# Reordering the matmul steps of a fused attention and FFN kernel's forward stage, and moving one weight load

## The chip, the cores and the metric

One NeuronCore of a Trainium2 chip runs the whole program. The metric is the device time of one execution in microseconds (us). The kernel before was run three times: 1677.09, 1677.39 and 1687.07 us, median 1677.39 us.

## The reference

The program computes a transformer block with attention and a gated FFN in parallel, and all its gradients. Sequence length S = 2048, width D = 448, 16 heads of 28, FFN width F = 1792, all in bf16.

```python
def _fwd_reference(A_x, A_wqkv, A_wo, B_x, B_w_gate, B_w_up, B_w_down):
    x = A_x
    xn = layernorm(x)
    # attention: softmax(q k^T * 28**-0.5) v, then @ wo ; FFN: (silu(xn@w_gate) * (xn@w_up)) @ w_down
    return x + attention(xn, A_wqkv, A_wo) + ffn(xn, B_w_gate, B_w_up, B_w_down)

_out, _vjp = jax.vjp(_f, A_x, A_wqkv, A_wo, B_w_gate, B_w_up, B_w_down)
_grads = _vjp(grad_out)
return (_out, *_grads)        # output 0, and the six gradients as outputs 1 to 6
```

## The kernel before

**Stages.** A short prologue normalises x and projects q, k, v of the first head group. Then comes the forward stage, which is what the change touches. A second stage computes the attention gradients and, between them, the output rows and the input gradients. A short last stage finishes the gradient of x.

**The forward stage** is a list of 256 steps, `(g, qc, kt)`: 4 groups of 4 heads, 4 blocks of 512 queries (`qc`), 16 tiles of 128 keys (`kt`). In each step TensorE makes the scores of one key tile for the four heads as two *score pairs* (L531; each pair is two matmuls that use 32 rows of the array and run at the same time). ScalarE takes the exponential of each pair (L535). A pair's scores lie in one of two PSUM buffers `s_ps`, so a pair must wait for the exponential of the pair two before it. The *weighted sum* `pv(i)` (L504 to L515) is four matmuls of 32 output rows that run at the same time and accumulate exp(scores) times v in `o_ps`, of which there is one buffer. At the last key tile `pv` calls `o_items` (L420), which has VectorE copy `o_ps` to `o_raw` (L423) and puts two jobs at the front of the filler queue: four transposes of `o_raw` (`tr`, L432) and the matmuls of `do` (L454).

**Fillers.** All other matmuls of this stage wait in a queue of jobs, each a list of (cost, function) pairs; the costs are constants of the source (0.216 for a matmul of 512 columns, 0.19 for 448). `fill(budget)` takes items in order until the budget is used up. At each step `pace` is the cost still in the queue divided by the number of steps left. The queue holds the FFN: 14 blocks `fc` of 128 FFN columns, each in 4 parts `sc` of 512 rows. A part runs the jobs `a` (4 matmuls, then tanh on ScalarE at L349 and three VectorE operations), `u` (4 matmuls, then two VectorE operations, L363 and L365), in parts 1 to 3 one weight gradient `dW` of the block before (16 matmuls), and `dh` (4 matmuls, then two VectorE operations at L373, a transpose DMA on SP and three writes to `hd_d` on the POOL queue, L378). Behind the FFN block come `weight_layout` calls (L250), which transpose weights through one staging tile; four of the twelve read `wq_sb`, the layout of w_qkv in the tile `W`. Projections for the next head group go to the front of the queue at `qc == 2`. All these jobs use three PSUM buffers `f_ps` in turn.

**The order of one step before**: score pair 0, fillers for 0.45 of the pace, score pair 1, `pv` of the step before, fillers for 0.55 of the pace. At `kt == 1` the `pv` is put off, so that `kt == 2` runs two of them; this leaves `o_raw` time to be copied.

**The load of w_down.** `load_w("wd", 1)` allocates the tile `W` again (the pool has one buffer) and issues one DMA of 1568 KB on the POOL queue (L493). Before, this is called at step 224, the first of `qc == 2` of the last group (L522). The tile is first read in the second stage by the first output row (L658).

Each engine runs its own instructions in program order, and so do the DMA queues of SP and POOL.

Of the kernel before, what the change touches and what calls it, by code (L numbers as in the profile page):

```python
# [22 lines left out]
G = 4  # L23
# [14 lines left out]
def kernel(  # L38
# [145 lines left out]
    def sp_layouts(g):  # L184
        for tq, dst in ((0, spq_d), (1, spk_d)):
            s_ = stg.tile([P, NT, P], BF16, name="sp_stage")
            sp.dma_start_transpose(out=s_[:], in_=qk_tiles[(g, tq)][:])
            pool.dma_start(out=dst[g], in_=s_[:].rearrange("p t c -> p (t c)"))
# [61 lines left out]
    def weight_layout(c, i):  # L250

        d0, dn = DCH[c]
        s_ = stg.tile([P, NT, P], BF16, name="sp_stage")
        n = NFC if i < 2 else 3 * G
        src = ((B_w_gate, B_w_up)[i][d0:d0 + dn, :] if i < 2
               else wq_sb[:dn, c].rearrange("p t g r -> p (t g r)"))
        sp.dma_start_transpose(out=s_[:, :n, :dn], in_=src)
        dst = wT_d[i] if i < 2 else wqT_d
        pool.dma_start(out=dst[:, :, d0:d0 + dn], in_=s_[:, :n, :dn])
# [6 lines left out]
    def fill(budget):  # L266

        while budget > 0.05:
            if not cur:
                if not queue:  # L270
                    return
                cur.extend(queue.popleft())
            cost, fn = cur.popleft()
            fn()
            budget -= cost
            left[0] -= cost

    def push(jobs, front=False):
        left[0] += sum(c for job in jobs for c, _ in job)
        if front:  # L280
            queue.extendleft(reversed(jobs))
        else:
            queue.extend(jobs)

    def proj_items(g):
        out = []
        for tq in range(3):
            for sc in range(4):
                box = {}

                def go(c, tq=tq, sc=sc, box=box):
                    if c == 0:
                        box["m"] = proj_unit(g, tq, sc, "dve")
                    box["m"](c)
                out.append([(MM, lambda c=c, go=go: go(c)) for c in range(4)])
        out.append([(0.0, lambda: proj_done(g))])
        return out
# [3 lines left out]
    def dW_items(fc):  # L301

        out = []
        for wi in range(3):
            box = {}

            def go(t, wi=wi, box=box):
                src = ffn[fc]
                if t == 0:
                    box["ps"] = ps_f.tile([P, 512], FP32, name="f_ps")  # L310
                acc = box["ps"]
                rhs = dy_sp if wi == 0 else xn_sp
                pe.matmul(acc[:, :D], lhsT=src[:, 12 * (t // 4) + 4 * wi + t % 4, :], rhs=rhs[:, t, :D],  # L313
                          start=(t == 0), stop=(t == NT - 1))
                if t < NT - 1:
                    return
                if wi == 0:
                    o = ftmp.tile([P, D], BF16, name="dwd_sb")
                    dve.tensor_copy(out=o[:], in_=acc[:, :D])
                    pool.dma_start(out=out_6[fc * P:(fc + 1) * P, :], in_=o[:])  # L320
                else:
                    w = dwT[wi - 1]
                    dve.tensor_copy(out=w[:, :D], in_=acc[:, :D])
                    o = ftmp.tile([P, 4, P], BF16, name="dw_o")
                    sp.dma_start_transpose(out=o[:], in_=w[:])
                    dst = (out_4 if wi == 1 else out_5)[:, fc * P:(fc + 1) * P]
                    pool.dma_start(out=dst[0:384].rearrange("(c p) f -> p c f", p=P), in_=o[:, 0:3, :])
                    pool.dma_start(out=dst[384:448], in_=o[:64, 3, :])
            out.append([(MMD, lambda t=t, go=go: go(t)) for t in range(NT)])
        return out  # L330
# [54 lines left out]
    ffn_list = []  # L385
    pend = []
    for fc in range(NFC):
        nxt = dW_items(fc)
        for sc in range(4):
            ffn_list += ffn_items(fc, sc, pend[sc - 1:sc] if sc else [])  # L390
        if 0 < fc < 13:
            ffn_list.append([(0.0, lambda k=fc - 1: weight_layout(k // 3, k % 3))])
        pend = nxt
    ffn_list += pend
    push(ffn_list)
# [87 lines left out]
    wtile = {}  # L483

    def load_w(nm, parts):

        t = wp.tile([P, NFC, D], BF16, name="W")
        src = {"wd": B_w_down.rearrange("(fc p) d -> p fc d", p=P), "wg": wT_d[0], "wu": wT_d[1], "wq": wqT_d}[nm]
        n = 3 * G if nm == "wq" else NFC
        wtile[nm] = t  # L490
        step = n // parts
        q = pool if nm == "wd" else sp
        out = [lambda i=i: q.dma_start(out=t[:, i:i + step, :], in_=src[:, i:i + step, :])  # L493
               for i in range(0, n, step)]
        return out
# [6 lines left out]
    pv_next = [0]  # L502

    def pv(i):  # L504
        g, qc, kt = steps[i]
        if kt == 0:
            o_cur["o"] = ps_o.tile([P, 512], FP32, name="o_ps")
        o_ps, v = o_cur["o"], v_tiles[g]
        e = eTs.pop(i)
        for hh in range(4):  # L510
            pe.matmul(o_ps[HP * hh:HP * (hh + 1), :], lhsT=v[:, kt, HP * hh:HP * (hh + 1)],  # L511
                      rhs=e[hh // 2][:, hh % 2, :], start=(kt == 0), stop=(kt == NT - 1),
                      tile_position=(0, HP * hh), skip_group_check=True)
        if kt == NT - 1:
            o_items(g, qc, o_ps)  # L515

    for i, (g, qc, kt) in enumerate(steps):
        if kt == 0 and qc == 1:
            push([[(0.0, lambda g=g: sp_layouts(g))]], front=True)
        if kt == 0 and qc == 2 and g + 1 < G:  # L520
            push(proj_items(g + 1), front=True)
        if kt == 0 and qc == 2 and g + 1 == G:  # L522
            load_w("wd", 1)[0]()
        qT, kT = qk_tiles[(g, 0)], qk_tiles[(g, 1)]
        pace = left[0] / (nst - i)
        eTs[i] = []
        for half in range(2):
            s_ps = ps_s.tile([P, 2, 512], FP32, name="s_ps")
            for j in range(2):
                r = HP * (2 * half + j)  # L530
                pe.matmul(s_ps[:, j, :], lhsT=kT[r:r + HP, kt * P:(kt + 1) * P],  # L531
                          rhs=qT[r:r + HP, qc * 512:(qc + 1) * 512],
                          start=True, stop=True, tile_position=(r, 0))
            e = ep.tile([P, 2, 512], BF16, name="eT")
            act.activation(out=e[:], in_=s_ps[:], func=ACT.Exp, scale=SCALE)  # L535
            eTs[i].append(e)
            if half == 0:
                fill(0.45 * pace)
            else:
                if i >= 1 and kt != 1:  # L540
                    while pv_next[0] <= i - 1:
                        pv(pv_next[0])
                        pv_next[0] += 1
                fill(0.55 * pace)
    while pv_next[0] < nst:
        pv(pv_next[0])
        pv_next[0] += 1
    fill(1e9)
    fst.close()
    bst.close()  # L550

# [401 lines left out]
```

## Time and profile before

| what | value |
|---|---|
| median of three runs | 1677.39 us |
| the profiled execution: time / span | 1683.64 us / 1681.9 us |
| mean granted TensorE clock | 0.952 |
| forward stage, first to last score pair | 49.5 to 751.1 us |
| exponentials of the forward stage (L535) | 512 of 1025 ns |
| TensorE busy, all | 1519.8 us (90%) |
| ScalarE busy, all | 1186.3 us (71%) |
| VectorE busy, all | 1131.8 us (67%) |

The span is what the profiler covers; 1.7 us of the execution's time lie around it. The clock is the share of full speed that TensorE was granted. TensorE's busy time is modelled and overlaps, so that starts of instructions say more than their durations: below, the distance from the start of one group of matmuls to the start of the next is what a group costs.

### The profile page before, as it was taken

To read this page: it belongs to the slowest core of one execution; us is meant where nothing else is said; L and a number is where in the kernel's file an instruction comes from. 1 tells how busy PE (TensorE), PEld (TensorE's weight loads), DVE (VectorE), ACT (ScalarE), POOL (GpSimd) and SP (SyncE) were. 2 spreads that over 40 slices of the span, in tenths; PEclk is the share of its full clock that TensorE was granted. 3 is DMA by queue.
4 is the path that set the end of the run, shared out by engine and by line. 5 is a ranking of instruction groups with operands and counts; after the bars stand their busy time and mean duration, and the time that the engine had idled before them with its cause. 6 is when DMAs were issued, how large, how long until landed. Compare 5 with 4: busy or idle time off the path is not lost. (4 is left out here: it accounts for less than half of the span.)

```text
span 1681.9 us, 32121 instructions
## 1 busy us (share of the span) xinstructions
PE 1519.8 (90%) x12176; PEld 600.7 (36%) x12176; DVE 1131.8 (67%) x1530; ACT 1186.3 (71%) x1346; POOL 400.9 (24%) x664
## 2 busy tenths in 40 slices
PE   3699999999999999696998999999989999999875
PEld 1132333333233333232443335443335433544352
DVE  6365555555555456345887788888878888888736
ACT  2497888888777678574776777777777777777611
POOL 4133334344234333421001101010102101111132
PEclk9699999999998899797999989999999999999998
DMA  4785658687866577548999999999999999999963
GB/s 126 145 181 115 133 121 169 140 169 118 157 131 130 124 136 148 138 93 231 214 208 212 196 175 196 207 196 208 206 202 194 202 202 179 175 195 195 175 239 100
DMA packets 682155, 285.13 MB, mean 170 GB/s; under 512 B 637792, under 2 KB 651088, under 8 KB 682000
## 3 DMA queue, kind: packets, MB, share of 16 engines
q1 hardware_dynamic: 653616, 215.74, 68.7%
q0 software_dynamic: 25808, 64.30, 15.4%
q10 hardware_dynamic: 2576, 3.04, 0.6%
q8 instruction: 95, 1.56, 0.4%
q14 instruction: 60, 0.49, 0.1%
HBM read 67.34 MB, written 63.44 MB: 78 GB/s over the span
## 5 line engine op out<-in xcount | busy, mean ns | idle before, releaser
L831 DVE TENSOR_TENSOR ds<-sd,E 128x1024 bf16<-128x1024 f32 x512 | 607.6, 1217 | 81.5 <-PE sd L814 34.2
L819 ACT ACTIVATE E<-sd 128x1024 bf16<-128x1024 f32 x512 | 520.1, 1031 | 193.4 <-PE sd L814 99.0
L535 ACT ACTIVATE eT<-s_ps 128x1024 bf16<-128x1024 f32 x512 | 518.2, 1025 | 159.8 <-PE s_ps L531 154.5
L801 PE MATMUL sd<-KV,QD 32*128 32x512 bf16 x1024 | 202.1, 391 | 19.2 <-DVE ds L831 8.1
L814 PE MATMUL sd<-KV,QD 32*128 32x512 bf16 x1024 | 202.9, 388 | 10.9 <-DVE ds L831 6.8
L694 PE MATMUL acc<-ds,Qsp 128*32 128x512 bf16 x1024 | 204.5, 395 | 1.2 <-DVE ds L831 1.2
L531 PE MATMUL s_ps<-qT,kT 32*128 32x512 bf16 x1024 | 204.7, 397 | 0.0
L694 PE MATMUL acc<-E,dOsp 128*32 128x512 bf16 x1024 | 204.3, 395 | 0.0
L339 PE MATMUL f_ps<-xnT,wgu 128*128 128x512 bf16 x448 | 135.9, 400 | 24.7 <-DVE w_sb L365 13.0
L378 POOL DMA_DIRECT2D hd_d<-fT x168 | 126.9, 769 | 40.9 <-DVE fT L363 24.9
L531 PEld LDWEIGHTS <-kT 32*128 32x128 bf16 x1024 | 48.2, 91 | 203.7 <-issue 201.7
L664 PE MATMUL aux<-W,ck 128*128 128x448 bf16 x448 | 106.6, 354 | 6.9 <-DVE dsT L730 6.9
L313 PE MATMUL f_ps<-xn_sp,f_sp 128*128 128x448 bf16 x448 | 110.6, 355 | 0.0
L709 POOL DMA_DIRECT2D dqkv_d<-dkv_o x64 | 39.2, 617 | 284.9 <-ACT dkv_o L700 284.8
L801 PEld LDWEIGHTS <-QD 32*128 32x128 bf16 x1024 | 50.2, 91 | 149.0 <-issue 140.5
L511 PE MATMUL o_ps<-eT,v_sp 128*32 128x512 bf16 x1024 | 101.7, 399 | 0.0
L730 DVE COPY dsT<-aux 128x512 bf16<-128x512 bf16 x128 | 54.3, 424 | 61.7 <-ACT dsT L728 61.7
L694 PEld LDWEIGHTS <-dOsp 128*32 128x32 bf16 x1024 | 50.3, 94 | 120.3 <-issue 117.3
L814 PEld LDWEIGHTS <-QD 32*128 32x128 bf16 x1024 | 69.4, 91 | 53.4 <-issue 34.2
L721 PE MATMUL aux<-ident_bf,ds 128*128 128x128 bf16 x1024 | 78.5, 219 | 11.0 <-DVE dq_acc L758 3.5
L743 PE MATMUL aux<-dsT,Ksp 128*32 128x512 bf16 x1024 | 78.3, 405 | 4.1 <-DMA dsT<-ds 2.5
L351 DVE SCALAR_TENSOR_TENSOR g<-t_sb,f_ps 128x512 f32<-128x512 f32 x56 | 38.4, 686 | 64.6 <-ACT t_sb L349 64.5
(130 smaller groups left out, 1803.1 us busy)
## 6 DMA issues: line engine op xcount, KB each, us to landing
hd_d<-fT POOLq DMA_DIRECT2D x168, 128.0 KB, 4.0
ck<-hd_d SPq DMA_DIRECT2D x32, 448.0 KB, 4.2
ck<-hd_d SPq DMA_DIRECT2D x16, 576.0 KB, 5.0
dsT<-ds SPq DMA_TRANSPOSE x384, 4.1
dq_c<-dqkv_d SPq DMA_DIRECT2D x8, 768.0 KB, 4.7
dqkv_d<-dkv_o POOLq DMA_DIRECT2D x64, 64.0 KB, 3.5
W<-wT_d SPq DMA_DIRECT2D x14, 224.0 KB, 3.9
out_dram<-dw_o POOLq DMA_DIRECT2D x28, 96.0 KB, 4.1
```

Of the source, the lines that this page charges most:

```text
L313: pe.matmul(acc[:, :D], lhsT=src[:, 12 * (t // 4) + 4 * wi + t % 4, :], rhs=rhs[:, t, :D], start=(t == 0), stop=(t == NT - 1))
L339: pe.matmul(st[name][:], lhsT=w(c), rhs=src[:, tsl, c, :], start=(c == 0), stop=(c == 3))
L378: pool.dma_start(out=hd_d[tsl, :, G + NFC * wi + fc, :].rearrange("k p s -> p k s"), in_=o[:, wi, :].rearrange("p (k s) -> p k s", k=4))
L511: pe.matmul(o_ps[HP * hh:HP * (hh + 1), :], lhsT=v[:, kt, HP * hh:HP * (hh + 1)], rhs=e[hh // 2][:, hh % 2, :], start=(kt == 0), stop=(kt ...
L531: pe.matmul(s_ps[:, j, :], lhsT=kT[r:r + HP, kt * P:(kt + 1) * P], rhs=qT[r:r + HP, qc * 512:(qc + 1) * 512], start=True, stop=True, tile_ ...
L535: act.activation(out=e[:], in_=s_ps[:], func=ACT.Exp, scale=SCALE)
L664: return [lambda n=n: pe.matmul(ps[:, :D], lhsT=t[:, n, :], rhs=w[:, n, :], start=(n == 0), stop=(n == NFC - 1)) for n in range(NFC)]
L694: pe.matmul(acc[r:r + HP, :], lhsT=src[:, qt, 64 * hp + HP * j:64 * hp + HP * j + HP], rhs=m[:, j, :], start=(qt == 0), stop=(qt == NT - 1 ...
L801: pe.matmul(s_ps[:, j, :], lhsT=q[HP * j:HP * j + HP, qt * P:(qt + 1) * P], rhs=kv[HP * j:HP * j + HP, kc * 512:(kc + 1) * 512], start=Tru ...
L814: pe.matmul(d_ps[:, j, :], lhsT=q[r:r + HP, qt * P:(qt + 1) * P], rhs=kv[r:r + HP, kc * 512:(kc + 1) * 512], start=True, stop=True, tile_p ...
L819: act.activation(out=E[k][:], in_=s_ps[:], func=ACT.Exp, scale=SCALE)
L831: dve.tensor_tensor(out=DS[k - 1][:], in0=d_ps[:], in1=E[k - 1][:], op=ALU.mult)
```

## The change

A forward step becomes: score pair 0, `pv` of two steps before, score pair 1, then all fillers of the step in one call `fill(pace)`. The special case at `kt == 1` is gone; the last two `pv` run after the loop. The load of w_down is no longer called at step 224 but is an item of cost 0 in the filler queue, behind the last FFN block's last `dh` and ahead of that block's three `dW` jobs.

```diff
@@ -390,6 +390,8 @@
             ffn_list += ffn_items(fc, sc, pend[sc - 1:sc] if sc else [])
         if 0 < fc < 13:
             ffn_list.append([(0.0, lambda k=fc - 1: weight_layout(k // 3, k % 3))])
+        if fc == 13:
+            ffn_list.append([(0.0, lambda: load_w("wd", 1)[0]())])
         pend = nxt
     ffn_list += pend
     push(ffn_list)
@@ -519,8 +521,6 @@
             push([[(0.0, lambda g=g: sp_layouts(g))]], front=True)
         if kt == 0 and qc == 2 and g + 1 < G:
             push(proj_items(g + 1), front=True)
-        if kt == 0 and qc == 2 and g + 1 == G:
-            load_w("wd", 1)[0]()
         qT, kT = qk_tiles[(g, 0)], qk_tiles[(g, 1)]
         pace = left[0] / (nst - i)
         eTs[i] = []
@@ -534,18 +534,15 @@
             e = ep.tile([P, 2, 512], BF16, name="eT")
             act.activation(out=e[:], in_=s_ps[:], func=ACT.Exp, scale=SCALE)
             eTs[i].append(e)
-            if half == 0:
-                fill(0.45 * pace)
-            else:
-                if i >= 1 and kt != 1:
-                    while pv_next[0] <= i - 1:
-                        pv(pv_next[0])
-                        pv_next[0] += 1
-                fill(0.55 * pace)
+            if half == 0 and i >= 2:
+                pv(i - 2)
+        pv_next[0] = max(0, i - 1)
+        fill(pace)
     while pv_next[0] < nst:
         pv(pv_next[0])
         pv_next[0] += 1
     fill(1e9)
+    assert 'wd' in wtile
     fst.close()
     bst.close()
```

## The prediction

> **What bounds the kernel now.** I began with the page's table of 40 slices: TensorE is at 9 tenths in nearly all of the forward stage, with a drop in the 17th slice, and its granted clock dips there too. Then I read who waited for whom on TensorE from 60 to 720 us, which names every hole of that stage.
>
> ```profile
> PE   3699999999999999696998999999989999999875
> PEclk9699999999998899797999989999999999999998
> PE f_ps L339 <- DVE w_sb L365: 13.0, 2, 12.8
> PE f_ps L432 <- DVE o_raw L423: 11.1, 6, 3.2
> PE f_ps L313 <- DMA f_sp<-fT: 2.9, 1, 2.9
> ```
>
> So apart from its start this stage is one unbroken row of matmuls with 27 us of holes, 12.8 of them in one. No score pair ever waited for ScalarE. A step is then as long as its matmuls and whatever lies between them. TensorE's timeline shows one step, from a score pair 0 to the next; the first column is the start:
>
> ```profile
> 670.53 0.39 PE L531 MATMUL s_ps<-qT,kT 32*128 32x512 bf16 x2
> 670.85 0.82 PE L339 MATMUL f_ps<-dyT,wdT 128*128 128x512 bf16 x3
> 671.61 0.39 PE L531 MATMUL s_ps<-qT,kT 32*128 32x512 bf16 x2
> 671.92 0.40 PE L511 MATMUL o_ps<-eT,v_sp 128*32 128x512 bf16 x4
> 672.25 1.04 PE L339 MATMUL f_ps<-xnT,wgu 128*128 128x512 bf16 x4
> 673.23 0.39 PE L531 MATMUL s_ps<-qT,kT 32*128 32x512 bf16 x2
> ...
> 784.65 0.39 PE L694 MATMUL acc<-E,dOsp 128*32 128x512 bf16 x2
> 784.98 0.39 PE L801 MATMUL sd<-KV,QD 32*128 32x512 bf16 x2
> ```
>
> From start to start the runs take 0.32, 0.76, 0.31, 0.33 and 0.98 us. Three filler matmuls take 0.76 and four 0.98, so one matmul is about 0.215 us and each run pays some 0.115 us besides, whatever its length: 0.76 - 3 x 0.215. A pair or a `pv` runs as one such matmul at a time and pays the same (0.32 - 0.215). The last two lines, from the second stage, are the only neighbours like the new `pv` followed by a score pair: 0.33 us, the same again.
>
> The big hole is read on three engines' timelines; the bracket is the idle time before the instruction and what ended it:
>
> ```profile
> 689.37 1.11 POOL L493 DMA_DIRECT2D W<-in_B_w_down_dram  x1 [31.00 <-DMA sp_stage<-W]
> 699.96 0.69 DVE L363 SCALAR_TENSOR_TENSOR fT<-g,f_ps 128x512 bf16<-128x512 f32 x1 [13.40 <-DMA hd_d<-fT]
> 701.30 1.87 PE L339 MATMUL f_ps<-xnT,wgu 128*128 128x512 bf16 x4 [12.81 <-DVE w_sb L365]
> ```
>
> The load of w_down stands on the POOL queue from step 224 on, but may not overwrite `W` until the last `weight_layout` has read it, which SP does only at 684.87. For 31 us the `hd_d` writes queued behind it don't go, the three `fT` buffers fill, VectorE stops at L363, the `f_ps` buffer isn't freed and TensorE stops.
>
> **The change part by part.** The sum is made against the profiled 1683.6 us, 0.4% above the median 1677.4; a saving of this size is the same on either.
>
> *Runs of matmuls.* By the code, a step before has five runs (four at the 16 steps with `kt == 1`, and at the first): 256 x 5 - 17 = 1263. After, it has four, less the two first `pv`: 1022. The matmuls themselves are the same. 241 x 0.115 = 27.7 us less. From the spread of the starts (0.10 to 0.12) it is 24 to 29 us. [...]
>
> *The hole.* With the load behind the last `dh`, step 250 by a walk through the filler queue with the source's costs, the last reader of `W` is some 14 steps in the past, and nothing blocks POOL. 12.8 us go, and with them the slow clock after it: the clock rows read 0.50 from 691 us and 1.00 again from 708, so about 6 us of matmuls ran at half speed, 2.9 us. Next late there would be nothing that TensorE shows: its next wait is 0.6 us at 740. I take 15.7 us; a shorter wait on a busy queue would leave 10, a smoother stage after it give 18.
>
> *The load itself.* It is queued on POOL behind the last three `hd_d` writes (2.2 us) and the `dw_o` writes before them, issues in 1.1 us, and lands 8.4 us later (its row in the DMA list). Behind it waits the `dwd_sb` write, for whose buffer nobody is in a hurry. Six steps of 2.6 us and the 24 us from the last score pair (751.1) to the first matmul with `W` (774.9) are 40 us against 12: nothing, by 27 us. If that cover were gone, each us late would be a us of TensorE in the second stage's start.
>
> *ScalarE.* Two exponentials now come close together. Back to back, two take 1.93 and three 2.86 us, so 0.93 each; with one tanh (0.5) in 4.4 steps ScalarE needs 2.0 us a step. The shortest new step, with the early pace of 1.07 by the code (five filler matmuls), is 0.32 + 0.33 + 0.32 + 0.115 + 5 x 0.215 = 2.16 us. ScalarE stays just behind TensorE: +1 us (0 to 4). Were each exponential to cost its 1.025 us alone, ScalarE would need 2.17 and the first 100 steps would gain nothing: +11.
>
> *tanh.* This is what the change adds. tanh follows both exponentials of its step on ScalarE's queue; before, an `a` that ended in the first portion had its tanh between them. Counted from the start of score pair 0: the pair is done at 0.4, the exponentials end near 1.5 (0.1 on, 1.02 long) and 2.45 (0.93 more), tanh near 3.0, and VectorE's five operations, 0.6 to 0.7 us apart, near 6.4. Behind these stand two waits of TensorE.
>
> First, at the end of each query block `o_raw` (0.68 us) is queued on VectorE behind what `a`, `u` and `dh` left there, and `tr` waits for it. Before, the six waits in the stage come to 11.1 us. By the same walk I looked at which job lies ahead of `tr` at each of the 15 boundaries. After the change an `a` ends one to two steps ahead at steps 32, 48, 80, 112, 160 and 224, where `tr` waits 2.5, 2.5, 2.1, 2.0, 1.1 and 2.0 us; at 96 a `dh` and a projection make it 1.0; the others have a `dW` ahead and wait 0 to 0.3, 1.1 in all. That is 14.2 us, 3 more; step 192 and 208, which cost 3.2 and 2.7 before, become free.
>
> Such a wait also costs clock. These rows are stretches of 1 us: length, TensorE busy, clock:
>
> ```profile
> 510.00:511.00 1.00, 1.00 (x7) 1.00 1.08 187
> 511.00:512.00 1.00, 0.04 (x1) 1.00 0.86 149
> 512.00:513.00 1.00, 0.10 (x1) 0.87 1.04 179
> 513.00:514.00 1.00, 1.00 (x4) 0.50 1.58 311
> 522.00:523.00 1.00, 1.00 (x4) 0.51 0.93 212
> ```
>
> A wait of 1.86 us and then 10 us at half speed: 5 us lost. Read the same way, the waits at 146, 467, 561 and 610 us lost 3.5, 1.5, 4.5 and 1.6, so 3.2 on average with this one. Five such before, six after: +3.2. [...] Together +6 us; if these waits fall as well as they can, -13; if three more boundaries wait, +20.
>
> Second, part 0 of an FFN block has no `dW` between its `u` and the next part's `u`, which needs the same `f_ps` buffer. Twelve matmuls lie between; with VectorE done at 6.4 us the walk gives three waits of 0.3 to 0.4 us: +1.5 (0 to 8).
>
> Sum: -27.7 - 15.7 + 1 + 6 + 1.5 = -34.9 us. 1677.4 - 34.9 = 1642.5; I say 1643.
>
> **Rivals.** (1) *ScalarE or a returning block takes a part*: exponentials don't overlap (+11), or POOL blocks elsewhere and the hole stays (+15.7; a 5.2 us wait of VectorE for `hd_d` at 455 us, with no w_down load near, shows that it can). 1654 to 1658. (2) *A `pv` between two score pairs pays the price of two runs*: removing one run then saves nothing, and only the hole goes, less the new waits: -15.7 + 8.5, 1670. Against it stands the equal 0.115 at all five places of the step and at the pair of the second stage. (3) *Slower: TensorE waits for VectorE behind the later tanh in every FFN block.* A wait costs 2 us and 3.2 of clock, 5.2. Thirteen block starts would cost 68, less the 1.5 counted: 1643 + 66 = 1709. It decides from seven such waits on (34.9 / 5.2). For it: the wait of 0.18 us that the trace shows at 650 for L339 on L365, so the margin before was near nothing; against it: three of thirteen by the walk, and short. (4) *It doesn't do what it says*: the load still waits, now at the end of the stage, on something that I don't see. It would then delay the second stage's start only beyond 27 us.
>
> **How the numbers follow.** The forecast, with its bounds (1630 to 1653), 0.57; rival 1, 0.15; rival 2, 0.17; rival 3, 0.09; rival 4, 0.02. About 1% (16.8 us) is what a measurement of this kernel can tell from no change. Faster by over 1% is the forecast and rival 1: 0.72. Within 1%: rival 2, half of rival 4: 0.18. Slower: rival 3 and the rest: 0.10. For 8 in 10 the range goes from 1630 to 1670, with rivals 1 and most of 2 in it; some 0.05 lie below, 0.14 above.
>
> **What would show it.** Right: four runs a step with about 0.115 us each, `pv` to score pair in 0.33; no wait of POOL at L493 and no hole near 690; last score pair near 716 us; the second stage as long as before; L432 waits of some 14 us at the boundaries named. Wrong: score pairs or `pv` that wait for the exponential, L339 waiting for L365 in most blocks, the first matmul with `W` waiting for its load, or a clock below 0.95 in the forward stage.

## The result, and the profile after

The changed kernel takes 1652.5 us (median of six runs, 1644.9 to 1664.6) where the kernel before takes 1679.8 (six runs). The ratio is 0.983, 95% interval 0.980 to 0.986, so 28 us less (23 to 33), 1.7%. Forecast were 34.9 us less and a time of 1643, with bounds from 1630 to 1653: the time lies at the upper bound, and a fifth of the forecast saving is missing.

The page of the changed kernel, its row of TensorE and of the granted clock, in 40 slices of its 1653.5 us span:

```profile
PE   3699999999999999969998989999989899999884
PEclk9799999999999999979999989999999999999888
```

The drop in the 17th slice is gone; the one in the 18th is the change of stage. Where the forward stage begins and ends is in the answer on the score pairs: the line gives the count, the shortest, median and longest duration in ns, and the first and last start.

```profile
L531 PE MATMUL s_ps<-qT,kT x1024: 384/385/605, 49.6 to 716.6; 32*128 32x512 bf16 x171
```

The last pair starts at 716.6 instead of 751.1 us, 34.5 less; the forecast was near 716. One step, on TensorE's timeline:

```profile
655.82 0.39 PE L531 MATMUL s_ps<-qT,kT 32*128 32x512 bf16 x2
656.14 0.40 PE L513 MATMUL o_ps<-eT,v_sp 128*32 128x512 bf16 x4
656.47 0.39 PE L531 MATMUL s_ps<-qT,kT 32*128 32x512 bf16 x2
656.79 1.04 PE L339 MATMUL f_ps<-xnT,wgu 128*128 128x512 bf16 x4
657.67 0.92 PE L313 MATMUL f_ps<-xn_sp,f_sp 128*128 128x448 bf16 x4
658.52 0.39 PE L531 MATMUL s_ps<-qT,kT 32*128 32x512 bf16 x2
```

Four runs, from start to start 0.32, 0.33, 0.32 and 1.73 us. The `pv` between two score pairs costs 0.33, as its neighbour in the second stage did. In this step only a change between kinds of matmul has the price: from the four matmuls of L339 to those of L313, which use the array in the same shape (128*128), it is 0.88 us, hardly more than 4 x 0.215, so both together are one run. Who waited on TensorE, from 60 to 716 us (total, times, longest):

```profile
PE f_ps L434 <- DVE o_raw L425: 11.0, 8, 2.2
PE f_ps L339 <- DVE w_sb L365: 8.6, 4, 4.1
PE f_ps L313 <- DMA f_sp<-fT: 5.2, 2, 2.8
```

(The transposes `tr` are L434 now, `o_raw` L425.) The waits for `o_raw` are as large as before, and elsewhere; L339 and L313 wait longer than forecast. The load of w_down does as forecast: on the POOL queue it starts without a wait, and its first use comes 35 us later.

```profile
705.16 1.10 POOL L495 DMA_DIRECT2D W<-in_B_w_down_dram  x1
740.42 0.58 PE L655 MATMUL aux<-W,ck 128*128 128x448 bf16 x1
```

For all kernels below, the forward stage is taken apart in the same way: when the last score pair starts; TensorE's idle time from 72 us to then; and the time lost to the clock, which is TensorE's busy time in each us times one less the granted clock. The runs are counted by the code. The kernels ran on three chips, on which the median of the kernel before was 1679.2 to 1681.8 us.

| kernel (label) | last pair | idle | lost to the clock | runs | median | ratio to before (interval) |
|---|---|---|---|---|---|---|
| before | 751.1 | 27.7 | 26.1 | 1263 | 1679.8 | |
| changed | 716.6 | 24.8 | 18.4 | 1022 | 1652.5 | 0.983 (0.980 to 0.986) |
| changed, again (c1) | 733.2 | 25.3 | 37.1 | 1022 | 1651.9 | 0.981 (0.976 to 0.985) |
| load moved only (e1) | 734.0 | 13.2 | 22.9 | 1263 | 1666.7 | 0.991 (0.988 to 0.993) |
| new steps, load at step 228 (e2) | 734.5 | 36.5 | 24.9 | 1022 | 1668.7 | 0.992 (0.989 to 0.994) |
| tr and do later (e3) | 697.6 | 16.8 | 7.2 | 1022 | 1629.9 | 0.971 (0.965 to 0.976) |
| five runs (e4) | 734.1 | 17.0 | 17.0 | 1278 | 1666.8 | 0.990 (0.986 to 0.993) |
| lag of one (e5) | 738.2 | 33.3 | 30.9 | 1023 | 1671.8 | 0.994 (0.991 to 0.996) |
| four fT (e6) | 713.2 | 17.3 | 23.6 | 1022 | 1642.8 | 0.977 (0.972 to 0.981) |
| e3 and e6 together (e7) | 690.9 | 11.7 | 5.5 | 1022 | 1620.8 | 0.964 (0.960 to 0.967) |
| e7 again (c2) | 689.1 | 11.3 | 4.9 | 1022 | 1625.9 | 0.969 (0.966 to 0.973) |
| e7, five runs (e8) | 706.1 | 1.8 | 3.6 | 1278 | 1638.4 | 0.976 (0.973 to 0.979) |
| old steps, moved, tr later (e9) | 710.3 | 4.3 | 7.9 | 1263 | 1642.3 | 0.977 (0.972 to 0.982) |

First pair to last, the stage fell from 701.6 to 667.0 us in the two profiles, by 34.6: 2.9 less idle, 7.7 less lost to the clock, and the other 24.0 for 241 fewer runs, 0.100 each. How exact such a remainder is, two executions of the changed kernel tell (changed and c1): the second's stage is 17.0 us longer, idle time and clock account for 19.2, and 2.2 us are left over, which is 0.009 us a run.

### The profile page after: what moved, and what is told of

Read it like the earlier page. It is cut to its first block, busy times and chain, and to the rows that moved or that the text cites. A ratio compares the mean times of both kernels' runs of the same rounds, so it can differ in the third digit from the quotient of the medians.

```text
span 1653.5 us, 32129 instructions
## 1 busy us (share of the span) xinstructions
PE 1489.1 (90%) x12176; PEld 620.8 (38%) x12176; DVE 1130.9 (68%) x1530; ACT 1167.4 (71%) x1346; POOL 400.7 (24%) x664
## 4 chain that ended last, share of the span: by engine, by line
PE 60%; DMA 12%; DVE 11%; ACT 8%; issue 6%; SPq 2%; POOL 1%; DVEq 0%; POOLq 0%; ACTq 0%
PE s_ps L531 9%; PE f_ps L313 8%; PE f_ps L339 8%; DMA dsT<-ds 7%; PE sd L798 5%; ACT E L816 5%; DVE ds L828 5%; PE o_ps L513 5%; PE aux L661 5%; PE acc L691 4%; PE aux L740 4%; PE aux L655 3%; PE f_ps L157 3%; PE sd L811 2%; ACT dsT L725 2%
## 5 line engine op out<-in xcount | busy, mean ns | idle before, releaser
L535 ACT ACTIVATE eT<-s_ps 128x1024 bf16<-128x1024 f32 x512 | 497.1, 1022 | 132.0 <-PE s_ps L531 130.4
L339 PE MATMUL f_ps<-xnT,wgu 128*128 128x512 bf16 x448 | 122.8, 391 | 20.4 <-DMA wd<-in_B_w_down_dram 11.8
L313 PE MATMUL f_ps<-xn_sp,f_sp 128*128 128x448 bf16 x448 | 101.6, 359 | 0.0
L718 PE MATMUL aux<-ident_bf,ds 128*128 128x128 bf16 x1024 | 78.6, 220 | 11.7 <-DVE dq_acc L752 4.3
L313 PEld LDWEIGHTS <-f_sp 128*128 128x128 bf16 x672 | 58.5, 98 | 73.5 <-issue 23.4
```

The source lines that it names most:

```text
L339: pe.matmul(st[name][:], lhsT=w(c), rhs=src[:, tsl, c, :], start=(c == 0), stop=(c == 3))
```

## Experiments on the two halves of the change

**The load alone (e1).** The steps of the kernel before, with this:

```diff
+        if fc == 13:
+            ffn_list.append([(0.0, lambda: load_w("wd", 1)[0]())])
...
-        if kt == 0 and qc == 2 and g + 1 == G:
-            load_w("wd", 1)[0]()
```

> The steps of the kernel before, with only the load of w_down moved behind the last FFN block's dh. My theory: POOL no longer waits 31 us at the load, the hole of 12.8 us before L339 and some 3 us of half clock after it go, the last score pair of the forward stage starts near 735.5 us instead of 751.1, and the time falls by 15.7 us (10 to 18). Rival: the hole was slack for what comes next, so other waits of TensorE take its place and the time falls by less than 6 us.

The last score pair came at 734.0, 17.1 us earlier; the time fell by 16 us (ratio 0.991, interval 0.988 to 0.993). Idle time fell by 14.5. The hole was a loss of its own and nothing else took its place. The rival falls.

**The steps, with the load where it blocks (e2).** The changed kernel, with the load taken out of the queue and called at a step:

```diff
-        if fc == 13:
-            ffn_list.append([(0.0, lambda: load_w("wd", 1)[0]())])
...
+        if i == 228:
+            load_w("wd", 1)[0]()
```

> The new steps, with the load of w_down called at the start of step 228, where the filler queue stands about where it stood at step 224 before (part 1 of FFN block 12 just begun). My theory: POOL blocks again until the last weight_layout has read W, TensorE gets a hole of some 12 us near 660 to 680 us, and the time is 12 to 18 us above that of the changed kernel, some 12 to 19 below before. Rival: if the runs of matmuls save nothing and all the gain is the hole's, this is as slow as before.

16 us above the changed kernel by the medians, and 14 below before. The block and the hole are back, on POOL's and TensorE's timelines:

```profile
672.02 1.11 POOL L493 DMA_DIRECT2D W<-in_B_w_down_dram  x1 [25.21 <-DMA sp_stage<-W]
```
```profile
683.32 1.87 PE L339 MATMUL f_ps<-xnT,wgu 128*128 128x512 bf16 x4 [11.71 <-DVE w_sb L365]
```

The rival falls. So each half is worth about as much as the other, and they add: -16 and -14 against -28. The load at step 224 itself wasn't tried with the new steps. By the walk through the queue, four parts of FFN block 12 would then still lie between TensorE and the last `weight_layout`, and there are three `fT` buffers: the load and the fillers would wait for each other. That is worked out from the code and not shown by a run; by it the new steps need the load some steps later than before, as here, or moved.

**Five runs again (e4).** The fillers split in two, everything else as changed:

```diff
-            if half == 0 and i >= 2:
-                pv(i - 2)
+            if half == 0:
+                fill(0.45 * pace)
+                if i >= 2:
+                    pv(i - 2)
...
-        fill(pace)
+        fill(0.55 * pace)
```

> The changed kernel, with the fillers split again into 0.45 and 0.55 of the pace: score pair 0, fillers, pv of two steps before, score pair 1, fillers: five runs a step instead of four, with the lag, the place of the load and the matmuls of the changed kernel. My theory: 256 more runs at 0.115 us, 29 us, less up to 8 us because tanh stands between the two exponentials again: 20 to 30 us above the changed kernel, near that of the move alone less nothing. Rival: the price is not per run but the gain comes from the lag of two steps or from the one portion's bookkeeping: within 6 us of the changed kernel.

14 us above the changed kernel by the medians: neither in my range nor in the rival's. The table tells why. First pair to last took 684.8 us against 667.0, 17.8 more, though idle time was 7.8 and the loss to the clock 1.4 lower. Without those the 256 runs cost 27.0 us, 0.105 each, a little under the 0.115 that I held. What I had too small is what the split gives back: fewer waits.

**The same with few waits (e8, e9).** e8 is e7 (below) with the edit of e4. e9 is e1 with `tr` and `do` put off as in e3.

> The kernel with late tr and do and four fT buffers, its fillers split again: five runs a step instead of four. With few waits left, little clock is lost by chance, so the difference shows the price of a run. By the two kernels with many waits it is 0.10 us: 255 runs, 24 to 29 us above the kernel with four runs, 1645 to 1650. Rival: that price was an accident of the waits and the clock, and the difference is under 10 us.

> The old steps (five runs, lag of one, double pv at kt 2) with the load moved and with tr and do two steps later. Against the new steps with late tr and do (1629.9 us) it has 241 runs more: 24 to 29 us above it, 1654 to 1659. Rival: the old order leaves more time to VectorE and has so few waits left that the new order gains less than 15 us over it.

> The kernel with late tr and do and four fT buffers once more, for these comparisons on one chip: 1617 to 1625 us, with a spread of its runs under 8 us because few waits are left.

By the medians e8 is 12 us above c2 on the same chip, and e9 16; against e3, on another chip, e9 is 12 above. e8 lies between my expectation and its rival's; e9 against e3 is what its rival said: the old order has fewer waits left. c2 lies just above its expected range, at 1625.9 us, and scatters by 10 us, not under 8. Again the idle time differs the other way: e8's forward stage has almost no idle time, 1.8 us against 11.3. First pair to last, e8 took 656.7 us and c2 640.4; with idle time and clock set equal the 256 runs cost 16.3 + 9.5 + 1.3 = 27.1 us, 0.106 each. For e9 against e3 it is 661.7 - 647.5 + 12.5 - 0.7 = 26.0 for 241, 0.108. Changed against e1 gives 17.4 + 11.6 - 4.5 = 24.5, 0.102. Four comparisons, 0.102 to 0.108 us a run, with 0.100 for the change itself: that price is settled to about 0.01. In each of the four pairs four runs a step also leave 8 to 13 us more idle time than five, so three tenths to a half of what the runs save is given back in waits.

## Experiments on the waits

**tr and do two steps later (e3).** `o_items` no longer pushes its jobs, but notes them for the step after next:

```diff
-        push([...] + (dwo_items(g) if qc == 3 else []), front=True)
+        late.append((step_now[0] + 2, jobs_o))
...
+        step_now[0] = i
+        while late and late[0][0] <= i:
+            push(late.pop(0)[1], front=True)
```

> The changed kernel, with the jobs tr, do and dwo put into the filler queue two steps later than o_items is called, so that o_raw has been copied when tr is reached. My theory: the waits of L434 on o_raw (11.8 us in nine) all but go, and with them the half clock after those above 1.2 us, so the time falls by 18 to 24 us against the changed kernel. Rival A: the half clock has other causes, and only the idle 11 us go. Rival B: VectorE's backlog is the limit, and the wait appears elsewhere (score pairs, pv, L339): less than 4 us.

1629.9 us, 21 (by the ratios) to 23 us (by the medians) below the changed kernel. TensorE's waits from 70 to 697 us in this kernel:

```profile
PE f_ps L339 <- DVE w_sb L365: 5.1, 3, 4.1
PE f_ps L313 <- DMA f_sp<-fT: 4.0, 2, 2.6
PE f_ps L157 <- DVE w_sb L365: 2.5, 1, 2.5
PE o_ps L515 <- DVE o_raw L425: 2.1, 3, 0.8
```

The line for `tr` is no longer there; 2.1 us of it moved to `pv`, which needs the `o_ps` buffer that `o_raw` is copied from. Against the first profile of the changed kernel idle time fell by 8.0 us and the loss to the clock by 11.2 (29.9 against its repeat, c1). Rival A, that only the idle time goes, falls: here the waits cost more in clock than in idle time. Rival B falls too.

**Four fT buffers (e6), and both (e7).** `fT` from three buffers to four, `eT` from seven to five for the space.

> The changed kernel with four fT buffers instead of three (and five eT buffers instead of seven, for the space; a lag of two steps needs five). My theory: the two holes of about 4 us before L339 come from VectorE waiting at L363 for an fT buffer whose DMAs are late, and go; 8 us of idle time and 3 to 5 of half clock, 8 to 13 us below the changed kernel. Rival: the late DMAs only block something else a little later: less than 4 us.

1642.8 us, 9 below the changed kernel beside it (c1). That is in the expected range, but the runs alone don't show it: four runs of each scatter by 12 and 24 us, and the two intervals in the table overlap. What the fourth buffer takes away is seen in the changed kernel on VectorE and then TensorE:

```profile
453.80 0.69 DVE L363 SCALAR_TENSOR_TENSOR fT<-g,f_ps 128x512 bf16<-128x512 f32 x1 [4.46 <-DMA hd_d<-fT]
```
```profile
455.14 1.01 PE L339 MATMUL f_ps<-xnT,wgu 128*128 128x512 bf16 x2 [4.14 <-DVE w_sb L365]
```

VectorE stands at L363 for a free `fT` buffer whose write to `hd_d` hasn't landed (in the other hole, up to 91.97 us, it waits 5.47 us for the transpose into `f_sp`), keeps its `f_ps` buffer, and TensorE stops: the chain of the w_down hole, but from DMAs that are merely late. With four buffers L339 waits less:

```profile
PE f_ps L434 <- DVE o_raw L425: 11.6, 8, 2.2
PE f_ps L313 <- DMA f_sp<-fT: 5.0, 3, 2.6
PE f_ps L339 <- DVE w_sb L365: 0.7, 2, 0.4
```

> Both: tr and do two steps later, and four fT buffers. If the two kinds of waits are independent, the gains add: 18 to 22 us from the first (measured) and 8 to 13 from the second, 1617 to 1625 us. If they share a cause in VectorE's backlog, no better than 1628.

1620.8 us, and 1625.9 on another chip: the fastest here, 3.1 to 3.6% below before (ratios 0.969 and 0.964 with the intervals of the table) where the change alone is 1.7 to 1.9% below. That is what independent gains would give, but no proof of it: on top of e3 the fourth buffer brought 4 to 9 us by the medians, within the scatter.

**A lag of one step (e5).** `pv(i - 1)` in the place of `pv(i - 2)`.

> The changed kernel with pv of one step before instead of two. pv then stands 0.32 us into a step and needs the second exponential of the step before, which ends near 2.45 us after that step's start, while early steps are 2.2 us long. My theory: pv waits 0.1 to 0.4 us in most of the first 100 steps and after each tanh, hardly in the last 100: 8 to 25 us above the changed kernel. Rival: ScalarE is never late, the lag of two steps buys nothing: within 4 us.

20 us slower than the changed kernel beside it, inside my range, but not by my mechanism. On TensorE's timeline the distance from score pair 0 to the `pv` behind it, which would hold such a wait, has the median 0.32 us and is never above 0.54, here as there. First pair to last is 20.6 us longer than in the first profile of the changed kernel: 8.5 is idle time (`tr` waits 17.8 us instead of 11.0, L313 for `f_sp` 9.7 instead of 5.2), 12.5 is clock, a term that differs by 18.7 between two profiles of the changed kernel itself. Why these waits grow with the lag, and whether it's more than other jobs falling ahead of `tr`, stays open.

**The changed kernel again (c1).**

> The changed kernel once more, beside the next three. My theory: the forward stage saves 34 to 35 us again, and the 6 us that the second and last stage took longer in its profile are chance, so the median lies near 1646 to 1652. Rival: the moved load or the earlier start lengthens the later stages by 6 us in every run.

1651.9 us; by the ratio 33 us below before on that chip (interval 25 to 41). The median is at the edge of my range, but the forward stage didn't save 34 to 35 us again: 17.9 in this profile. The rival's longer later stages don't show either (918.7 us from the first score pair of the second stage to the end, against 922.2 in the first profile and 915.7 before). The profile fell on a long run, 1668.6 us, and is the most telling of all: the waits are the same as in the first profile, to a few tenths, and the last score pair came at 733.2, 16.6 us later. Compare one wait, the same 2.23 us before L434 in both. First the changed kernel, then the repeat; the columns are the stretch, its length, TensorE busy, the clock, and the DMA's share and GB/s:

```profile
180.00:190.00 10.00, 7.77 (x51) 0.93 0.77 206
190.00:200.00 10.00, 10.00 (x67) 0.90 0.28 67
200.00:210.00 10.00, 10.00 (x61) 1.00 0.49 104
```
```profile
180.00:190.00 10.00, 7.77 (x50) 0.91 0.93 216
190.00:200.00 10.00, 10.00 (x44) 0.50 0.27 66
200.00:210.00 10.00, 10.00 (x51) 0.74 0.38 78
```

After the one the clock is slow for about 3 us, after the other for some 17: 1.7 us lost against 8.5.

## Why the prediction was right, and where it was off

*Runs of matmuls* (forecast -27.7): right, and a little too large. The runs measure 0.100 to 0.108 us rather than 0.115; 241 of them are -24 to -26, at the low end of the stated 24 to 29.

*The hole* (-15.7): right. The load alone brought 17.1 us in the forward stage and 16 in the time. "Next late there would be nothing" held: e1 has no new wait.

*The load itself* (0): right; the first matmul with `W` came 35 us after the load's issue and waited only for `ck`, as before.

*ScalarE* (+1): right. The trace of before has tanh (L349) at 0.59 us rather than the 0.5 of the sum, which leaves ScalarE's need at 2.0 us a step. No score pair and no `pv` is listed as waiting for an exponential in any kernel of the table up to its last score pair (the list begins at 0.15 us).

*tr at the block boundaries* (idle +3): the walk through the queue named the places well. Forecast at steps 32, 48, 80, 96, 112 and 224 were 2.5, 2.5, 2.1, 1.0, 2.0 and 2.0 us; measured 2.23, 2.23, 1.59, 0.74, 1.80 and 2.08. At 160 1.1 was forecast and none came; the hole of 4.14 us at L339 ended just before. 192 and 208 became free.

*Part 0 of the FFN blocks* (+1.5, 0 to 8): too small. L339 waits 8.6 us, of which 8.0 are two holes with a cause that I had read in the profile of before (VectorE waiting 5.2 us for `hd_d`) and put into a rival rather than into the sum: `fT` buffers that are late. e6 shows it. The two waits of L313 for `f_sp`, 5.2 us against 3.5, weren't foreseen either and are not explained.

*The clock* (+0.3 for the whole: -2.9 and +3.2): this is the term that was mis-sized. I took 3.2 us for every wait as if it were a price. In the two profiles of the changed kernel the same waits lost 18.4 and 37.1 us; in the profile of before 26.1. By the first the term is -7.7, by the second +11.0. So the 34.5 us at the end of the forward stage, equal to the forecast, is partly luck: runs 3.7 and idle time 4.4 worse than forecast, clock 8.0 better. With the clock of the repeat it is 17.9.

The medians lie between them, 28 us in one comparison and 33 in the other. The two profiled executions themselves differ by 28.2 us: the 34.5, less 6.4 that the first profile of the changed kernel took longer from the first score pair of the second stage to the end (922.2 against 915.7 us). The other profiles lie there from 913.8 to 921.1, the repeat of the changed kernel at 918.7, so most of the 6.4 is scatter; that a few us of it come from the change isn't excluded.

Of the rivals, ScalarE as the bound and the price of two runs for a `pv` in the middle fell. The slower one, VectorE behind the later tanh in every FFN block, showed its mechanism only at the boundaries and didn't spread. The fourth, a load that still waits, fell too: it starts without a wait.

## What to carry to other kernels

Count how often the tensor engine changes between kinds of matmul, price a change from starts in the timeline (0.100 to 0.108 us here), and group work to have fewer; then look at which queues the regrouped work now arrives at in one lump, since here three tenths to a half of the saving came back as waits. The load that had to wait for the last reader of its buffer kept POOL idle for 31.00 us before and 25.21 in e2, with the `hd_d` writes behind it, and TensorE waited 12.81 and 11.71 us; put such a load behind that reader in the program. Where one job needs a copy just ordered on another engine, put it off by a step or two: that edit and one more buffer brought 27 to 31 us more, about as much as the whole change.

## What the runs showed of the hardware

A wait of TensorE can cost more in clock than in idle time, and not in proportion to its length: the hole of 12.8 us lost 3.0 us afterwards, waits of 1.8 to 2.3 us lost between 1.7 and 13.7 (the last in e6, at 103 us), and waits of 2.4 us in e7 and 2.5 in c2, both near 680 us, lost nothing. The wait of 1.6 us at step 80 lost nothing in three executions (changed, e2, e6) and 6.8 us in the repeat. Four runs of e3, e7, c2 or e8, which have few waits, scatter by 7 to 10 us, six of the changed kernel by 20. But e9, with 4.3 us of idle time, scatters by 14, so the waits don't explain all of it.

The clock records kept with the traces show steps. In all thirteen traces each slow stretch (granted clock 0.50) that begins between 72 us and the last score pair lasts a whole multiple of 3.41 us: 27 last one, 21 two, 11 three and 6 from four to eight of these steps. Within a trace all of them begin and end on one grid of 3.41 us, and the grid lies elsewhere in each execution: counted from the start of the span, modulo a step, at 0.74 us before, 0.82 in the changed kernel, 1.97 in e2, 3.09 in c2. Of the two stretches compared under c1, the first is one step (188.56 to 191.97 us) and the second five (188.12 to 205.19). That the same wait costs one step or five, with TensorE busy throughout behind it, isn't explained by the grid alone and stays open.
